# First batch's softmax with tokens on partitions, sums by pairs of heads, six float32 steps

## The chip, the cores and the metric

One core of one Trainium2 chip. The metric is the device time of one execution in microseconds, the median of the runs of the kernel. The engines are named as in the profile: PE is TensorE (PEld its weight loads), DVE is VectorE, ACT is ScalarE, POOL is GpSimd, SP is SyncE, whose queue issues nearly all transfers.

## The reference

Memory attention of 8 batches, 8 heads, 576 tokens, head dimension 64, 32 memories, followed by a feed-forward layer (512 to 2048 to 512) on the 4608 tokens. All in float32.

```python
a = exp(phi - max over the 576 tokens);  a = a / (sum over the tokens + 1e-9)
k_m = einsum('bhsm,bhsd->bhmd', a, k);   v_m = einsum('bhsm,bhsd->bhmd', a, v)
scores = q @ k_m^T / 8;                  attn = softmax over the 32 memories
x = attn @ v_m, heads side by side       # 4608 x 512
h = x @ w_in;  g = h * erf(softplus(h));  out = g @ w_out
```

## The kernel before

The work is a sequence of 128 steps: 8 batches times 16 chunks of 128 of the 2048 hidden columns. For each batch v_m is first multiplied with w_in ("vw"), so that a step's h is one product of the attention weights (`at`, 256 head-memory rows by 576 tokens) with vw. A step consists of:

- `ffn1`: h of the chunk, two halves of 288 tokens (`U`), each 2 float32 matmuls in the first `FR1` = 4 steps ("exact") and 6 afterwards, where each operand is split into a rounded high part and a rest (float32r), three products for each of two groups of 128 rows;
- `softplus` and `erf` on ACT, in groups of four steps, because each needs its own table;
- `g_split` on DVE: g = e*h, and from step `FR2` = 8 on also a high part and a rest of it;
- `ffn2`: g's columns times w_out, added up in four PSUM banks (`pso0` to `pso3`) over the 16 steps of a batch, one float32 matmul for each bank in the first `FR2` steps, three split ones afterwards. The last 64 tokens of two batches are done together (`ffn2_rest`, tile `psr`). `store` copies a bank out on ACT and issues the transfer.

w_in and w_out come as packed 64-bit words (`load_weight`), and `decode` restores float32 with one ACT and two DVE operations; `split_wo` makes the split of w_out for the later steps.

Each operation is put on a list with an engine (or several to choose from), a cost and a rank (`op`). `Plan.order` then simulates the engines with these costs and issues, engine by engine, the ready operation of lowest rank. So the order in each engine's queue is fixed before the run and follows the planner's costs. `at(step)` is 100 times the step; some ranks and engines are corrected by a table of numbers just before the plan is run. Where the planner sees PE idle before the first second product, `fill` puts matmuls of an identity there (tile `idle`, L378). Tiles come from pools of few slots, and an operation waits until a slot is free; PSUM has four slots in the pool `ps`.

The first batch's start, before: the transposed phi is loaded (`phiT`), its maxima, exponentials and sums are taken along the tokens (`phi_sums`), and PE turns the exponentials so that tokens lie on partitions (`numbers_of`). The sums over the tokens for k and v (`sums_and_turn`, L619) are matmuls with phi's 32 columns of one head as weights, four heads beside each other in the array, and k's (or v's) 64 columns streamed. ACT or DVE scales the result by 1/sum while copying it twice (tile `kvk`), PE turns it (L651), and it is copied to `km` or `vm`. Scores (`attention`, L689) have the memories on partitions: km is the weight, q is streamed, 288 tokens in a unit, two units. DVE transposes blocks of 32 by 32 (L737), so that softmax runs over the 32 memories along the free dimension: maximum (L740), subtraction (L742), exp on ACT (L745), sum (L746), reciprocal, product (L751), and the block transposition back (L758) into `at`.

Transfers are issued in the order phiT (two halves), k (two groups), first half of q, first w_in, v (two groups), second half of q, second w_in, first w_out, and so on. q's halves lie in two of the eight slots of the pool `wo`, which the weights take over later.

Of the kernel before, what the change touches and what calls it, by code (L numbers as in the profile page):

```python
# [9 lines left out]
F32 = mybir.dt.float32  # L10
# [21 lines left out]

ROW = 116

PE, DVE, ACT, POOL, SP = "PE", "DVE", "ACT", "POOL", "SP"
# [39 lines left out]
class Plan:  # L75
# [55 lines left out]
    def order(self):  # L131
# [29 lines left out]
        while len(out) < len(self.ops):  # L161
# [70 lines left out]
            for y in x.after:  # L232
                n_wait[y] -= 1
                y.ready = max(y.ready, x.end + self.SIGNAL)
                if not n_wait[y]:
                    for w in y.ways:
                        waiting[w].append(y)
# [10 lines left out]
def tile_memory_attention_then_erf_softplus_ffn(  # L248
# [5 lines left out]
    phi: bass.AP,  # L254
    phiT: bass.AP,
    w_in: bass.AP,
    w_out: bass.AP,
# [27 lines left out]
    LAG = 6  # L285
    FR1, FR2 = 4, 8
    IN_PSUM = 1

    pools = {
# [60 lines left out]
    make_identity(nc, ident)  # L350
    begun = const.tile([P, 1], F32, name="begun")
    rest = const.tile([P, NK, 2, P], F32R, name="rest")
    km = [const.tile([P, NP_, M], F32, name=f"km{i}") for i in range(2)]
# [64 lines left out]
    def load_q(rank, u):  # L418
        b, hf = divmod(u, 2)
        src = qT[b, hf].rearrange("r (p s) -> r p s", p=NP_)  # L420
        if u < 2:
            key = tile_("wo", "q", u, shape=[P, NP_, U], pool="wo")
            load(rank, P * NP_ * U * 4, [key], lambda: nc.sync.dma_start(out=get(key), in_=src))
            return
        for x in range(2):
            key = tile_("at", "q", u, x, shape=[P, 2, U], pool="at")
            load(rank, P * 2 * U * 4, [key], lambda x=x, key=key: nc.sync.dma_start(
                out=get(key), in_=src[:, 2 * x : 2 * x + 2]))

    def q_keys(u):  # L430
        return [("q", u)] if u < 2 else [("q", u, x) for x in range(2)]

    def q_of(u, rows, p):
        return get(("q", u))[rows, p] if u < 2 else get(("q", u, p // 2))[rows, p % 2]

# [101 lines left out]
    def memories(rank, rank_2, b, parts):  # L537
# [5 lines left out]
        else:  # L543
# [5 lines left out]
            for g in range(NG):  # L549
                numbers_of(rank, b, g, range(n, NC), last, g)  # L550
        for turn_n, part in enumerate(parts):
            first, second = sums_and_turn(rank_2 + turn_n * 0.01, b, part)
            together(rank_2 + turn_n * 0.01, first)
            together(rank_2 + turn_n * 0.01, second)

    bundles = []
# [165 lines left out]
    def attention(rank, rank_2, u, more=0):  # L722
# [13 lines left out]
        for g in range(NG):  # L736
# [15 lines left out]
            out=view(), in0=view(), in1=wide(rs), op=ALU.mult))  # L752
        shape = [P, NG, U]
        if u < 2:
            to = tile_("at", "at", u, shape=shape, pool="at")
        else:
            to = tile_("sc", "f", u)
        op(DVE, on_dve(S), rank_2, [s], [to], lambda: nc.vector.transpose(  # L758
            out=get(to).rearrange("p g n -> p (g n)"), in_=get(s).rearrange("p g n -> p (g n)")))
        if u >= 2:  # L760
            at_split(rank_2, u, to)

# [11 lines left out]
    def ffn1(rank, i, half):  # L774
# [4 lines left out]
        part = [(k % 4, par) for par in range(2)]  # L779
        h = ("h", i)  # L780
        if i < IN_PSUM:
            ps = tile_(f"pso{half + 1}", "psh", i, half)
        else:
            if half == 0:
                tile_("h", *h)
            ps = tile_("ps", "psh", i, half, shape=[P, U], pool="ps")

        def emit():
# [10 lines left out]

        op(PE, (2 if exact else 6) * mm(U, exact), rank, [(w, q) for w in ws for q in part] + ats,  # L800
           [ps], emit, holds=[] if i < IN_PSUM else [h])
        if i < IN_PSUM:
            return

        def keep():
            return get(h)[:, half * U : (half + 1) * U]

        op(DVE, on_dve(U), rank - 20, [ps], [(h, half)],
           lambda: nc.vector.tensor_copy(out=keep(), in_=get(ps)),  # L809
           other={ACT: (on_act(U, True), lambda: nc.scalar.activation(keep(), get(ps), AF.Identity))})  # L810

    last = []

    def halves_of(i):

        return [(slice(x * U, (x + 1) * U), ("psh", i, x)) for x in range(2)]

    def softplus(rank, i, edge):
        e = tile_("e", "e", i)
        if i < IN_PSUM:  # L820
            for x, (half, ps) in enumerate(halves_of(i)):
                last[:] = [op(ACT, on_act(U, True), rank, [ps], [(e, x)],
                              lambda half=half, ps=ps: nc.scalar.activation(
                                  get(e)[:, half], get(ps)[:, :U], AF.Softplus),
                              kind="softplus", edge=edge and x == 1, after=last)]
            return
# [8 lines left out]
    def g_split(rank, i):  # L835
# [3 lines left out]
        if i < FR2:  # L839
            t = tile_(("g_hi", "g_lo")[i % 2], "g", i, shape=[P, S], pool="g")  # L840
            if i < IN_PSUM:
                for x, (half, ps) in enumerate(halves_of(i)):
                    op(DVE, on_dve(U), rank, [(e, x), ps], [(t, x)],
                       lambda half=half, ps=ps: nc.vector.tensor_tensor(
                           out=get(t)[:, half], in0=get(e)[:, half], in1=get(ps)[:, :U], op=ALU.mult))
# [27 lines left out]
    def ffn2(rank, i, d):  # L873
# [8 lines left out]
        def emit():  # L882
# [4 lines left out]
           kind="stop filling" if k == 0 else None)  # L887
        if k == NK - 1:
            store(rank, o, [(b * S + d * P, P)])

    def ffn2_rest(rank, b, first, n):
# [14 lines left out]
        if first + n == NK:  # L906
            store(rank, o, [((b + x) * S - REST, REST) for x in range(2)])

    def store(rank, o, rows):
        final = o[1] >= B - 2 if o[0] == "psr" else o[1] == B - 1  # L910
# [3 lines left out]
        for n, (r, ln) in enumerate(rows):  # L914
            e, by = (ACT, nc.scalar) if o == ("psr", B - 1) and n else (SP, nc.sync)
            op(e, 60, rank, [t], [], lambda n=n, r=r, ln=ln, by=by: by.dma_start(
# [34 lines left out]
    decode(at(-3), "in", 0)  # L951
    for u in range(2):
        together(at(-8), attention(at(-8), at(-7 + 2 * u), u))
    together(at(-5), vw(at(-5), 0, 0, 2, FR1 > 0))
# [6 lines left out]
    for c in range(NPR):  # L961
        if c:
            when(2 * c - 3, decode, at(2 * c - 3), "in", c)
            n = at(2 * c - 1.5)
            when(2 * c - 1, lambda n=n, c=c: together(n, vw(n, 0, 2 * c, 2, 2 * c < FR1)))
        when(2 * c, decode, at(second[2 * c] - 2.5), "out", c)
        n = second[16 + 2 * c] - 5 - c if 2 * c < FR2 else second[2 * c] - 2
# [63 lines left out]
    for b in range(1, B, 2):  # L1031
        for k in range(0, NK, 2):
            n = (b + 1) * NK + 2 + k // 4 if b < B - 1 else max(second[NS - NK + k + 1] + 1, NS)
            when(n, ffn2_rest, at(n + 0.6), b, k, 2)
    for k in range(NS):
        when(split_at[k], g_split, at(second[k] - 1.5), k)
        for d in range(NT):
            when(second[k], ffn2, at(second[k] + 0.5), k, d)

# [14 lines left out]
    for n, d in {  # L1054
        104: -18, 161: 366, 162: 366, 180: -354, 217: 211, 229: -211, 253: -495,
    }.items():
        plan.ops[n].rank += d
    for n, e in {103: ACT, 174: ACT}.items():
        plan.ops[n].ways = {e: plan.ops[n].ways[e]}
# [64 lines left out]
```

## Time and profile before

| | |
|---|---|
| median of 3 runs | 705.66 us (705.51 to 705.80) |
| profiled execution | 705.09 us |
| its span, first to last instruction | 703.3 us |
| granted clock of PE, mean | 0.999 |
| PE / PEld / DVE / ACT / POOL busy | 695.2 / 561.2 / 450.1 / 492.1 / 108.7 us |
| bytes moved | 66.71 MB, mean 95 GB/s |

How to read the rows: a timeline row has start, duration, engine, line, operation, output and inputs by the program's names, shapes, count of merged instructions, and in brackets the idle time before it and who ended it. A row of a group has count, busy time and mean nanoseconds of one. A row of stretches has the stretch, its length, and each engine's busy time with its count, then the granted clock, the DMA engines' share and GB/s. A float32 matmul stands in the trace as two records of PE and two of PEld, a float32r one as one of each. A q behind an engine's name is its queue, which issues transfers. Matmul durations overlap, so the distance from start to start tells their cost.

### The profile page before, as it was taken

How to read it: one execution, taken by the hardware profiler on the slowest of the kernel's cores; microseconds unless marked ns; L12 is line 12 of the kernel's file. 1: busy time of each engine (PE TensorE's matmuls, PEld its weight loads, DVE VectorE, ACT ScalarE, POOL GpSimd, SP SyncE). 2: the span in 40 equal slices, each digit the busy share in tenths (PEclk: the TensorE clock that was granted, in tenths of full speed). 3: DMA queues.
4: the chain of work that ended last, by engine and by line, in shares of the span. 5: the costliest groups of instructions: out<-in, count | busy, mean ns of one | idle time of the engine just before them, and what ended most of it. 6: DMA issues, size and time to landing. Idle time of an engine off the chain costs nothing.

```text
span 703.3 us, 12316 instructions
## 1 busy us (share of the span) xinstructions
PE 695.2 (99%) x4858; PEld 561.2 (80%) x4858; DVE 450.1 (64%) x775; ACT 492.1 (70%) x796; POOL 108.7 (15%) x262
## 2 busy tenths in 40 slices
PE   8999999999999999999999999999999999999997
PEld 4665678888887888888888788888888788888886
DVE  4999999678753576775554755765575346745530
ACT  4899989966866777888655876687576555776821
POOL 0031223211110211111111111111111021111110
PEclk9999999999999999999999999999999999999999
DMA  9999130714202041123310323110010100010002
GB/s 362 417 414 416 70 101 3 285 35 180 73 3 81 29 188 41 57 65 104 119 34 1 108 83 140 35 61 1 5 62 4 61 16 1 2 60 1 1 1 75
DMA packets 19849, 66.71 MB, mean 95 GB/s; under 512 B 2256, under 2 KB 2256, under 8 KB 19792
## 3 DMA queue, kind: packets, MB, share of 16 engines
q1 hardware_dynamic: 19424, 64.85, 24.8%
q10 hardware_dynamic: 368, 1.08, 0.4%
q8 instruction: 38, 0.62, 0.4%
q14 instruction: 19, 0.16, 0.1%
HBM read 56.49 MB, written 9.44 MB: 94 GB/s over the span
## 4 chain that ended last, share of the span: by engine, by line
PE 90%; ACT 5%; DMA 3%; DVE 1%; issue 1%; ACTq 0%
PE pso L869 49%; PE psh L792 27%; PE psr L869 6%; PE psa L689 5%; PE psa L619 2%; DMA q<-qT 2%; ACT w L448 1%; ACT e L832 1%; ACT e L827 1%; ACT L832 1%; ACT vw_hi L365 1%; DMA phiT<-phiT 1%; DMA out<-ot 0%; ACT ot L913 0%; PE psa L651 0%
## 5 line engine op out<-in xcount | busy, mean ns | idle before, releaser
L869 PE MATMUL pso<-wo,g_hi 128*128 128x512 f32 x960 | 301.0, 395 | 0.2 <-ACT ot L913 0.2
L869 PEld LDWEIGHTS pso<-wo,g_hi 128*128 128x128 f32 x960 | 171.7, 188 | 44.2 <-issue 12.6
L869 PE MATMUL pso<-wo,g_lo 128*128 128x512 f32 x480 | 188.5, 393 | 0.0
L810 ACT ACTIVATE h<-psh 128x288 f32<-128x288 f32 x175 | 71.4, 409 | 136.9 <-PE psh L792 135.9
L865 POOL CAST rest<-g_hi 128x64 fp32r<-128x64 f32 x120 | 54.9, 458 | 430.7 <-DVE g_hi L860 415.2
L860 DVE CAST g_hi<-e 128x576 fp32r<-128x576 f32 x120 | 53.9, 451 | 95.4 <-PE pso L869 93.7
L792 PE MATMUL psh<-at_hi,vw_hi 128*128 128x288 f32 x496 | 110.1, 303 | 0.3 <-DVE vw_lo L367 0.3
L869 PEld LDWEIGHTS pso<-wo,g_lo 128*128 128x128 f32 x480 | 90.1, 188 | 20.5
L792 PE MATMUL psh<-at_lo,vw_hi 128*128 128x288 f32 x496 | 106.3, 296 | 0.0
L792 PE MATMUL psh<-at_hi,vw_lo 128*128 128x288 f32 x496 | 105.8, 295 | 0.0
L858 DVE TENSOR_TENSOR e<-e,h 128x576 f32<-128x576 f32 x120 | 89.2, 755 | 21.8 <-ACT e L832 21.8
L792 PEld LDWEIGHTS psh<-at_hi,vw_hi 128*128 128x128 f32 x496 | 87.2, 188 | 17.9 <-issue 4.5
L861 DVE TENSOR_TENSOR g_lo<-e,g_hi 128x576 fp32r<-128x576 f32 x120 | 92.6, 772 | 7.6
L827 ACT ACTIVATE e<-h 128x576 f32<-128x576 f32 x127 | 86.0, 684 | 6.0 <-DVE h L809 3.8
L832 ACT ACTIVATE e<-e 128x576 f32<-128x576 f32 x128 | 81.0, 677 | 0.4
L792 PEld LDWEIGHTS psh<-at_hi,vw_lo 128*128 128x128 f32 x496 | 79.8, 188 | 0.0
L792 PEld LDWEIGHTS psh<-at_lo,vw_hi 128*128 128x128 f32 x496 | 79.2, 188 | 0.0
L865 POOL CAST rest<-g_lo 128x64 fp32r<-128x64 f32 x120 | 44.1, 367 | 92.8 <-DVE g_lo L861 89.8
L367 DVE TENSOR_TENSOR vw_lo<-psa,vw_hi 128x512 fp32r<-128x512 f32 (+1 forms) x68 | 40.1, 637 | 15.0 <-ACT vw_hi L365 15.0
L869 PE MATMUL psr<-wo,rest 128*128 128x512 f32 x192 | 49.3, 392 | 0.0
L809 DVE COPY h<-psh 128x288 f32<-128x288 f32 x79 | 35.3, 450 | 16.6 <-PE psh L792 16.1
L365 ACT ACTIVATE vw_hi<-psa 128x512 fp32r<-128x512 f32 (+1 forms) x68 | 34.1, 561 | 12.4 <-PE psa L689 12.3
(81 smaller groups left out, 653.8 us busy)
## 6 DMA issues: line engine op xcount, KB each, us to landing
kv<-kv SPq DMA_DIRECT2D x31, 640.0 KB, 8.3
out<-ot SPq DMA_DIRECT2D x32, 256.0 KB, 2.2
w<-w_in SPq DMA_DIRECT2D x8, 1023.8 KB, 15.0
w<-w_out SPq DMA_DIRECT2D x8, 1023.8 KB, 14.8
q<-qT SPq DMA_DIRECT2D x28, 288.0 KB, 3.2
phi<-phi SPq DMA_DIRECT2D x7, 640.0 KB, 4.4
phiT<-phiT SPq DMA_DIRECT2D x15, 288.0 KB, 3.3
q<-qT SPq DMA_DIRECT2D x2, 576.0 KB, 10.3
```

The lines of the kernel that those rows point to most:

```text
L365: lambda: nc.scalar.activation(get_hi(), get_src(), AF.Identity))
L367: lambda: nc.vector.tensor_tensor(out=get_lo(), in0=get_src(), in1=get_hi().bitcast(F32), op=ALU.subtract))
L792: nc.tensor.matmul(out=get(ps)[:, :U], lhsT=x[:, g, k % 4 * P : (k % 4 + 1) * P], rhs=y[:, g, :], start=(n + g == 0), stop=(n == len(parts ...
L809: lambda: nc.vector.tensor_copy(out=keep(), in_=get(ps)),
L810: other={ACT: (on_act(U, True), lambda: nc.scalar.activation(keep(), get(ps), AF.Identity))})
L827: last[:] = [op(ACT, on_act(S), rank, [("h", i)], [e], lambda: nc.scalar.activation(get(e), get(("h", i)), AF.Softplus), kind="softplus", ...
L832: last[:] = [op(ACT, on_act(S), rank, [e], [e], lambda: nc.scalar.activation(get(e), get(e), AF.Erf), kind="erf", edge=edge, after=last)]
L858: op(DVE, on_dve(S), rank, [e, h], [e], lambda: nc.vector.tensor_tensor(out=get(e), in0=get(e), in1=get(h), op=ALU.mult))
L860: op(DVE, on_dve(S, 1), rank, [e], [hi], lambda: nc.vector.tensor_copy(out=get(hi), in_=get(e)))
L861: op(DVE, on_dve(S), rank, [e, hi], [lo], lambda: nc.vector.tensor_tensor(out=get(lo), in0=get(e), in1=get(hi).bitcast(F32), op=ALU.subtract))
L865: lambda x=x, y=y: nc.gpsimd.tensor_copy(out=rest[:, k, x, cols], in_=get(y)[:, NT * P :]))
L869: nc.tensor.matmul(out=o, lhsT=y, rhs=z, start=(start and n == 0), stop=(stop and n == len(parts) - 1))
```

## The change

- First batch's sums: k's (v's) 128 columns of a pair of heads are the weights, phi's 64 columns of the pair are streamed; the useful blocks lie on the diagonal, so nothing is turned. 1/sum comes from a diagonal matrix multiplied by ones on PE ("every"), copied to SBUF; one DVE operation for each parity of heads and group multiplies and writes km or vm. km is written into a cleared 128 x 256 area beside the first part of q, zero outside the blocks.
- First batch's attention: q comes as 256 and 320 tokens. Three units: 256 tokens (two blocks of 128), 128 tokens, 192 tokens (two blocks of 96). q is the weight and km is streamed, so tokens lie on partitions and softmax needs no block transposition. For unit 0 (`AGAIN`) the scores are computed a second time and minus the maximum is added by a matmul, so that ACT takes exp directly from PSUM; for the other two DVE subtracts. PE turns the result, and ACT or DVE copies it to `at`.
- `FR2` is 6 instead of 8. The exact first products have halves of 256 and 320 tokens, the second in pieces of 32 and 288.
- The last three steps' second products are issued bank by bank (`TAIL`), the last bank is copied in two halves by ACT and DVE and stored through both queues.
- In the planner PE work that follows PE work is ready without the signal's delay; the table of corrected ranks has 50 entries instead of 7, that of engines 7 instead of 2.

```diff
-    FR1, FR2 = 4, 8
+    FR1, FR2 = 4, 6
+    AGAIN = (0,)
+    TAIL = 3
...
+    def first_memories(rank):
...
+        for x in range(2):
+            ps = tile_("ps", "psa", "mem", x, shape=[P, NP_, 2, M], pool="ps")
+            for g in range(NG):
+                def sums(ps=ps, x=x, g=g):
+                    for p in range(2):
+                        for c, ln in enumerate(ROWS):
+                            pair = 2 * g + p
+                            nc.tensor.matmul(
+                                out=get(ps)[:, pair].rearrange("p e m -> p (e m)"),
+                                lhsT=get(("kv", 0, x, g))[:ln, c, p * 2 * D : (p + 1) * 2 * D],
+                                rhs=get(a)[:ln, c, pair * 2 * M : (pair + 1) * 2 * M],
...
+                op(PE, 2 * NC * mm(2 * M, True), rank + x * 0.01, [a, ("kv", 0, x, g)], [(ps, g)], sums)
...
+    def first_attention(rank, rank_2):
...
+        for unit, (t0, n, nc_) in enumerate(((0, P, 2), (2 * P, P, 1), (3 * P, (S - 3 * P) // 2, 2))):
...
+            op(PE, nc_ * NP_ * mm(2 * M, True), rank, [qk] + kms, [ps], scores)
+            op(DVE, on_dve(w), rank_2, [ps], [mx], ... reduce_max ... negate=True
+            if unit in AGAIN:
...
+                op(PE, nc_ * NP_ * mm(2 * M, True), rank_2, [qk] + kms, [ps_2], ... scores(ps_2, False))
+                op(PE, mm(w, True), rank_2, [ps_2, mx], [ps_2], less)
+                op(ACT, on_act(w, True), rank_2, [ps_2], [e], ... AF.Exp
+            else:
+                op(DVE, on_dve(w), rank_2, [ps, mx], [e], ... add
+                op(ACT, on_act(w), rank_2, [e], [e], ... AF.Exp
...
+            op(PE, NG * nc_ * 108, rank_2, [e], [pt], turn)
...
-        op(PE, (2 if exact else 6) * mm(U, exact), rank, [(w, q) for w in ws for q in part] + ats,
+        op(PE, 2 * mm(n, True) + 70 * half if exact else 6 * mm(U, False), rank,
...
+    def halves(i):
+        at_ = 2 * P if i < FR1 else U
+        return slice(0, at_), slice(at_, S)
...
+            if b == B - 1 and k >= NK - 4:
+                n, rank = second[NS - 1], at(second[NS - TAIL] + 0.5) + 10 * (k - NK + 4) / 2 - 0.5
...
+            late = k - (NS - TAIL)
+            when(second[k], ffn2, at(second[k] + 0.5) if late < 0 else at(second[NS - TAIL] + 0.5) + 10 * d + late, k, d)
```

More of the change, by code (lines that the diff above doesn't have):

```diff
@@ L779, in ffn1 @@
         part = [(k % 4, par) for par in range(2)]
-        h = ("h", i)
+        h, c = ("h", i), halves(i)[half]
+        n = c.stop - c.start
         if i < IN_PSUM:
@@ L785, in ffn1, with emit_first @@
                 tile_("h", *h)
-            ps = tile_("ps", "psh", i, half, shape=[P, U], pool="ps")
+            ps = tile_("ps", "psh", i, half, shape=[P, n], pool="ps")
+        def emit_first():
+            x, done = get(ws[0]), 0
+            while done < n:
+                v, a = divmod(c.start + done, U)
+                ln = min(n - done, U - a)
+                for g in range(NG):
+                    nc.tensor.matmul(
+                        out=get(ps)[:, done : done + ln], lhsT=x[:, g, k % 4 * P : (k % 4 + 1) * P],
+                        rhs=get(("at", v))[:, g, a : a + ln], start=g == 0, stop=g == NG - 1)
+                done += ln
         def emit():
@@ L805, in keep @@
         def keep():
-            return get(h)[:, half * U : (half + 1) * U]
-        op(DVE, on_dve(U), rank - 20, [ps], [(h, half)],
+            return get(h)[:, c]
+        op(DVE, on_dve(n), rank - 20, [ps], [(h, half)],
            lambda: nc.vector.tensor_copy(out=keep(), in_=get(ps)),
-           other={ACT: (on_act(U, True), lambda: nc.scalar.activation(keep(), get(ps), AF.Identity))})
+           other={ACT: (on_act(n, True), lambda: nc.scalar.activation(keep(), get(ps), AF.Identity))})
     last = []
+    def halves(i):
+        at_ = 2 * P if i < FR1 else U
+        return slice(0, at_), slice(at_, S)
     def halves_of(i):
-        return [(slice(x * U, (x + 1) * U), ("psh", i, x)) for x in range(2)]
+        return [(x, x.stop - x.start, ("psh", i, n)) for n, x in enumerate(halves(i))]
     def softplus(rank, i, edge):
@@ L820, in softplus @@
         if i < IN_PSUM:
[L821 to L824, printed above, removed]
+            for x, (half, n, ps) in enumerate(halves_of(i)):
+                last[:] = [op(ACT, on_act(n, True), rank, [ps], [(e, x)],
+                              lambda half=half, n=n, ps=ps: nc.scalar.activation(
+                                  get(e)[:, half], get(ps)[:, :n], AF.Softplus),
                               kind="softplus", edge=edge and x == 1, after=last)]
@@ L841, in g_split @@
             if i < IN_PSUM:
[L842 to L845, printed above, removed]
+                for x, (half, n, ps) in enumerate(halves_of(i)):
+                    op(DVE, on_dve(n), rank, [(e, x), ps], [(t, x)],
+                       lambda half=half, n=n, ps=ps: nc.vector.tensor_tensor(
+                           out=get(t)[:, half], in0=get(e)[:, half], in1=get(ps)[:, :n], op=ALU.mult))
             else:
```

169 lines of the change are left out of this document (147 added, 22 removed), and 7 rows, old and new, of the table g.

## The prediction

> **What bounds the kernel now.** I read the page's busy times first, then the chain of waits, then busy times by stretch.
>
> ```profile
> span 703.3 us, 12316 instructions
> PE 695.2 (99%) x4858; PEld 561.2 (80%) x4858; DVE 450.1 (64%) x775; ACT 492.1 (70%) x796; POOL 108.7 (15%) x262
> PE 90%; ACT 5%; DMA 3%; DVE 1%; issue 1%; ACTq 0%
> 22.27:38.97 16.70, 16.16 (x115) 11.13 (x113) 16.63 (x24) 16.32 (x29) 0.00 (x0) 1.00 1.02 415
> 38.97:63.00 24.03, 23.72 (x200) 15.11 (x198) 23.60 (x36) 23.88 (x39) 9.18 (x14) 1.00 1.02 414
> 63.00:110.00 47.00, 46.83 (x292) 32.01 (x291) 46.95 (x75) 40.89 (x65) 10.07 (x13) 1.00 0.35 130
> 0.00:22.27 22.27, 12.47 (x28) 5.59 (x28) 1.00 0.93 375
> ```
>
> The three stretches list PE, PEld, DVE, ACT, POOL, the clock and the DMA; the last row is the filling of L378 alone (PE, PEld). From 38.97 us, the first second product, PE is full. Before 22.27 more than half of what PE does is filling. So the time is the start, plus PE's work, plus the tail; DVE is full too from 22 to 110 us (46.95 of 47.00), which is a second bound close behind. The granted clock is 1.00 throughout. The profiled execution took 705.09 us for its span of 703.3; the median of the runs is 705.66. The sum below starts from 705.09, and 0.57 is added at its end.
>
> The start, in order of time:
>
> ```profile
> 7.96 1.33 PE L619 MATMUL psa<-kv,phi 116*32 116x64 f32 x80
> 10.83 0.29 DVE L678 TENSOR_SCALAR km<-psa 64x128 f32<-64x128 f32 x1 [0.73 <-ACT km L676]
> 10.85 1.04 PE L689 MATMUL psa<-q,km 64*32 64x288 f32 x16
> 11.82 3.49 PE L378 MATMUL idle<-ident 128*128 128x512 f32 x8
> 12.85 0.75 DVE L740 TENSOR_REDUCE smx<-sc 128x18 f32<-128x576 f32 x1
> 16.19 0.77 PE L619 MATMUL psa<-kv,phi 116*32 116x64 f32 x40 [0.17 <-DMA kv<-kv]
> 17.70 0.72 PE L689 MATMUL psa<-q,km 64*32 64x288 f32 x16 [0.75 <-DMA q<-qT]
> 19.16 0.95 PE L689 MATMUL psa<-w_in,vm 64*32 64x256 f32 x16
> 21.39 0.77 DVE L758 STREAM_TRANSPOSE at<-sc 128x576 f32<-128x576 f32 x1
> 22.50 2.10 PE L792 MATMUL psh<-at,vw_hi 128*128 128x288 f32 x8
> 26.27 0.77 DVE L758 STREAM_TRANSPOSE at<-sc 128x576 f32<-128x576 f32 x1
> 27.10 4.15 PE L792 MATMUL psh<-at,vw_hi 128*128 128x288 f32 x16
> 33.70 0.64 PE L792 MATMUL psh<-at_hi,vw_hi 128*128 128x288 f32 x2
> 37.10 0.59 PE L378 MATMUL idle<-ident 128*128 128x256 f32 x2
> 38.97 3.60 PE L869 MATMUL pso<-w,g 128*128 128x512 f32 x8
> ```
>
> The reader sees a chain: k sums, k memories, scores, softmax on DVE, the first product of step 0's first half at 22.50, its second half at 27.10, the first second product at 38.97.
>
> **The part that decides: the price of a narrow float32 matmul.** A float32 matmul is two records, each with its own weight load. The new sums load 128 columns of kv and stream 64 of phi; the new scores load up to 128 tokens and stream 64. No row has that shape. Two rows bound it:
>
> ```profile
> 64.00 0.30 PEld L869 LDWEIGHTS pso<-w,g 128*128 128x128 f32 x2 [0.47 <-issue]
> L869 PEld LDWEIGHTS pso<-wo,g_hi 128*128 128x128 f32 x960 | 171.7, 188 | 44.2 <-issue 12.6
> ```
>
> Low end: the 80 records at 7.96 run four column groups side by side, so 64 columns stream in 1.33/20 = 0.066 us. High end: after a stall two loads of 128 columns take 0.30 with 0.19 each, so the second starts 0.11 after the first, when the first matmul takes its weights over. If that holds here, a record cannot come more often than 0.11, and streaming hides beneath the loading. The second row has the very operation and width, so I take 0.11, that is 0.22 per matmul, and keep 0.13 for the range.
>
> ```profile
> 18.36 0.44 PE L651 MATMUL psa<-ident,kvk 128*128 128x128 f32 x2
> 56.71 0.66 PE L651 MATMUL psa<-ident,kvk 128*128 128x128 f32 x4
> 699.02 0.60 ACT L913 ACTIVATE ot<-psr 128x512 f32<-128x512 f32 x1 [0.76 <-PE psr L869]
> ```
>
> Two turns more take 0.22 more, so one is 0.11; ACT takes 0.60 for 512 columns out of PSUM.
>
> **PE's work to the first second product, at 0.22.** From 7.96: k sums 2 x 2 x 5 = 20 matmuls, 4.4, to 12.3; a wait for the two DVE products into the memory, bounded by 0.29 each (they have half of that row's columns), 0.65 with signals, to 13.0. Unit 0's scores 8 x 0.22 = 1.75; the same again, 1.75; the product that adds minus the maximum, 512 columns in two records of at most 0.45 (3.60/8 in the row at 38.97), 0.9. v sums 4.4. Unit 1's scores 0.87; unit 2's, with 96 columns loaded, 8 x 2 x 0.08 = 1.3. Turns: 10 at 0.11, 1.1. First vw 0.95. That is 25.9 if nothing waits. Then the exact first products of steps 0 to 3. Before: 32 records, 16 of them 4.15, so 8.3 less the drain, 7.8. The new halves are 256 and 320 tokens, the latter as 32 + 288; the columns are the same, but the four records of 32 columns take 0.11 instead of 0.03 each, +0.33 a step, 9.1 in all: 35.0. Two more vw (26.41 to 27.10 and 31.27 to 31.87 now) 1.3, steps 4 and 5 as now (33.70 to 36.96) 3.3, and the 0.9 of the fourth vw with phi's turn: 40.4 against 38.97. So the start is **+1.4**: the PE work added by the change, some 11 us, uses up the filling that it had. Bounds: at 0.13 the chain of DVE decides instead (rival one), -2.0; with a wait in PE's queue +4 (rival two).
>
> The chains beside it at 0.22: unit 0's numbers. Scores end 14.9, maximum over 512 columns 0.67 (0.75 for 576), the added product ends 17.5, exp 0.6, sum 0.67, small ones 0.4, product 0.68, turn and copy 1.2: 21.2, about 1 us ahead of the row at 21.39 + 0.77. This gain is real but covered by PE, which is still at v's sums (they end near 21.7). On DVE the change takes away ten operations of about 0.76 (rows at 12.85 and 21.39), four short transposes and the small ones, some 10.5; it puts in twelve of 0.34 to 0.68 and ten short ones, by the same rows and the 0.29 some 9: an estimate of 1.5 saved.
>
> DMA: q of the first batch keeps its bytes, split 256/320 tokens; the second part still ends the same sum of bytes, so unit 1 cannot start before the 17.70 of now. The k memory lies in the first q's slot; so the third w_out load, which takes that slot over, waits for unit 2's scores, and SP's queue behind it with it:
>
> ```profile
> 22.61 0.33 SPq L399 DMA_DIRECT2D w<-w_out  x1
> w<-w_out SPq DMA_DIRECT2D x8, 1023.8 KB, 14.8
> ```
>
> It is issued at 22.61 and lands 14.8 later, with that much transfer ahead of it, so 2 us of delay are hidden: nothing. Without that backlog they would be paid in full. POOL's clearing of the memory stands where POOL is idle (x0 in the stretch after): nothing; if it came late the products on DVE would wait.
>
> **Six float32 steps, not eight.**
>
> ```profile
> 65.92 3.43 PE pso L869 x8
> 94.08 2.75 PE pso L869 x12
> L860 DVE CAST g_hi<-e 128x576 fp32r<-128x576 f32 x120 | 53.9, 451 | 95.4 <-PE pso L869 93.7
> L861 DVE TENSOR_TENSOR g_lo<-e,g_hi 128x576 fp32r<-128x576 f32 x120 | 92.6, 772 | 7.6
> 121.93 1.22 DVE L367 TENSOR_TENSOR wo<-wf,wo 128x1024 fp32r<-128x1024 f32 x1
> 123.06 0.79 DVE L861 TENSOR_TENSOR g_lo<-e,g_hi 128x576 fp32r<-128x576 f32 x1
> 124.14 0.62 PE L869 MATMUL pso<-wo,g_hi 128*128 128x512 f32 x2
> ```
>
> PE: a float32 step is 3.43, a split one 2.75: 2 x 0.68 = **-1.4**, all of it where PE is full. DVE gets 2 x (0.45 + 0.77) = 2.4 more, and the split of w_out 3 (1.22) comes forward from 121.93 to some 85 us: 3.7 in a stretch where DVE is full, with 0.3 to spare at 123.85 (124.14 less the end of 123.06 + 0.79). Cover: 1.5 saved at the start, and ACT's 6 us of room between 63 and 110, to which the copies of h can go (47.00 less 40.89). Bounds 0 and +2; I take **+0.3**.
>
> **Later waits, ranks, tail.** Of PE's waits after 38.97 the longest are
>
> ```profile
> PEld psh L792 <- DVE vw_lo L367: 0.9, 2, 0.5
> PEld psa L619 <- ACT phi L534: 0.8, 1, 0.8
> 699.65 0.55 ACTq L916 DMA_DIRECT2D out<-ot  x1
> ```
>
> PE comes 1.4 later to them, and the ranks written out are other ones: -0.9 to +0.5, I take **-0.5**. At the end the order of the last three steps changes and no matmul is added; three stores go out earlier, the last copy is two halves of 256 columns instead of 512 (0.60 to about 0.4), queued on ACT and SP as now: -0.6 to 0, **-0.3**. If DVE still had work there, its half would wait.
>
> Sum: +1.4 - 1.4 + 0.3 - 0.5 - 0.3 = -0.5: 704.6, and 0.57 more for the median, 705.1; I give **705.0**. A measurement of this kernel tells about 0.2%, 1.4 us, from no change, so this is called no change.
>
> **Rivals.** One: *the narrow matmuls stream faster than their loads suggest*, 0.13 each or less. Then k sums end at 10.6, unit 0's numbers at 17.9, v (landed by 16.19) sums, first vw and its copy at 20.1, so the first product comes 2.3 earlier than 22.50, the second half near 25.5 instead of 27.10: start -2.0, with the other terms 701.7. For it: the 0.066 of the four groups, and PE's filling of 3.49 at 11.82, which shows room. Against it: the pair of loads. The Trainium skill, "TensorE: Matmul & The Clock Gate", section "Back-to-back issue gap", gives a gap of N/2.4 + 2.5 ns, from which I estimate some 0.056 us for a record of two passes of 64 columns, and by it the sum would be about 701.5; the 0.11 above speaks against it, and no run here shows 64 columns under such a load.
>
> Two, the other side: *a turn stands in PE's queue ahead of the first products*. PE runs in order; the turn of unit 2 waits for DVE's chain on it (0.67 + 0.68 + 0.67 + 0.4 + 0.68, and exp 0.6: 3.7) behind its scores. If unit 2's turn or the sums behind unit 0's stand before the first vw, PE waits 3.7 less the 1.0 that lies between: +2.7, 707.7. It decides as soon as over 1 us of it is not covered. For it: all of it is one queue, and scores have one rank. Against it: PE's filling of 12.47 shows that waiting is planned where it is cheap.
>
> Three: *DVE becomes the bound at steps 12 to 16*, because of its 3.7 more and 0.3 of room: +1.7 instead of +0.3, 706.4. Against it: the room on ACT.
>
> **Chances.** The forecast 0.45 (its own range 703.6 to 706.4: faster 0.15, same 0.25, slower 0.05); rival one 0.25, faster; two 0.15 (slower 0.13, same 0.02); three 0.15 (same 0.09, slower 0.06). Faster 0.40, within 0.2% 0.36, slower 0.24. Range 701.6 to 707.8: it takes in rival one's time and rival two's.
>
> **What the changed profile would show.** The sums: L619's successor with 40 records per memory; starts 0.11 apart, k sums of 4.4 us, mean I right; 2.2 to 2.7, rival one. The first product of step 0 at 24 to 26 us, the first second product near 40. Two steps fewer of float32 records (48 instead of 64), 2.75 for steps 6 and 7. PE waiting for DVE's g_lo between 105 and 125: rival three. PE's load idle before a turn, with DVE's product as releaser, between 18 and 29: rival two. The last store's copy of 256 columns about 4 us before the end. I am wrong if the first second product comes well ahead of 38.97, or later than 42.

## The result, and the profile after

The changed kernel takes 710.84 us (median of 5 runs, 710.73 to 711.09) against 705.66 of the kernel before (705.49 to 705.84): ratio 1.0077, 95% interval 1.0066 to 1.0088. That is 5.2 us slower; 705.0 was forecast, with a range of 701.6 to 707.8. Its profiled execution took 711.09 us for a span of 709.3 us, at a granted clock of 1.00.

From the page, the span, the busy times and the chain:

```profile
span 709.3 us, 12253 instructions
...
PE 701.2 (99%) x4824; PEld 575.6 (81%) x4824; DVE 449.0 (63%) x781; ACT 496.8 (70%) x805; POOL 106.0 (15%) x264
...
PE 94%; DVE 3%; ACT 2%; issue 0%; POOL 0%; POOLq 0%
```

PE is busy 99% of the time, as before. This share hides what happened, since PE's own filling and its matmuls' slow pitch count as busy. The timeline of PE up to the first second product tells more (start, duration, engine, line, output and inputs, count, idle time before):

```profile
9.05 4.58 PE L595 MATMUL psa<-phi,kv 116*128 116x64 f32 x40
...
14.30 3.78 PE L851 MATMUL psa<-q 128*128 128x64 f32 x32 [0.40 <-issue]
...
18.83 4.58 PE L595 MATMUL psa<-phi,kv 116*128 116x64 f32 x40
...
23.24 2.42 PE L851 MATMUL psa<-q 128*128 128x64 f32 x24
...
28.55 1.13 PE L942 MATMUL psh<-at,vw_hi 128*128 128x256 f32 x4 [0.33 <-ACT at L906]
...
30.60 1.67 PE L386 MATMUL idle<-ident 128*128 128x512 f32 x4
...
46.78 3.70 PE L1035 MATMUL pso<-w,g 128*128 128x512 f32 x8
```

These are the k sums, unit 0's scores (twice), the v sums, the other units' scores, the first product of step 0 (22.50 before), a filling, and the first second product (38.97 before). Forty records of 64 columns take 4.58, so one starts every 0.11 us. The first second product is 7.8 us later, where 1.4 was forecast.

DVE in the same stretch, and then the whole stretch from the first instruction to the first second product (its length, PE, PEld, DVE, ACT, POOL, clock, DMA share, GB/s):

```profile
13.74 0.95 DVE L611 SCALAR_TENSOR_TENSOR q<-psa,bias 64x64 f32<-64x64 f32 x4 [5.38 <-PE psa L595]
...
16.33 0.69 DVE L859 TENSOR_REDUCE smx<-psa 128x16 f32<-128x512 f32 x1 [1.64 <-PE psa L851]
...
23.44 0.48 DVE L611 SCALAR_TENSOR_TENSOR vm<-psa,bias 64x64 f32<-64x64 f32 x2 [3.82 <-PE psa L595]
...
23.95 0.69 DVE L879 TENSOR_REDUCE ssm<-sc 128x16 f32<-128x512 f32 x1
...
42.46 0.49 DVE L971 COPY h<-psh 128x320 f32<-128x320 f32 x1 [0.48 <-PE psh L942]
```

```profile
0.00:46.78 46.78, 42.85 (x318) 33.66 (x318) 29.46 (x58) 24.70 (x45) 0.99 (x8) 1.00 0.98 397
```

The kernel before, DVE's first operation on scores and its only longer wait behind it, then the whole stretch:

```profile
11.97 0.85 DVE L737 STREAM_TRANSPOSE sc<-psa 128x288 f32<-128x288 f32 x2 [0.84 <-PE psa L689]
...
18.50 0.85 DVE L737 STREAM_TRANSPOSE sc<-psa 128x288 f32<-128x288 f32 x2 [1.09 <-PE psa L689]
```

```profile
0.00:38.97 38.97, 35.86 (x363) 21.26 (x363) 28.80 (x49) 25.66 (x48) 0.70 (x6) 1.00 0.97 392
```

DVE does 29.46 us of work to that point, 28.80 before: about the same. But it waits 5.38 us for the k sums, 1.64 for the scores and 3.82 for the v sums. From its first operation on scores to the first second product DVE is full in both kernels, but for these waits:

| | before | after | difference |
|---|---|---|---|
| first operation of DVE on scores | 11.97 | 16.33 | +4.36 |
| idle from there to the first second product | 1.09 | 3.82 + 0.48 | +3.21 |
| work in that stretch | 25.91 | 26.15 | +0.24 |
| first second product | 38.97 | 46.78 | +7.81 |

The work is the stretch less its idle time. Counted from the beginning of the k sums, which is 1.09 later itself (9.05 for 7.96), the beginning of DVE's work on the scores is 3.27 later. From the first second product to the end of the last matmul it is 658.9 us now (to 705.7) and 660.0 before (to 698.98): -1.1. From there to the end of the span it is 3.6 and 4.3: -0.7. Sum +6.0, the difference of the two profiled spans; the medians differ by 5.2.

### The profile page after: what moved, and what is told of

Same layout as the page of the kernel before. It is cut to its first block, busy times and chain, and to the rows that moved or that the text cites. A ratio compares the mean times of both kernels' runs of the same rounds, so it can differ in the third digit from the quotient of the medians.

```text
span 709.3 us, 12253 instructions
## 1 busy us (share of the span) xinstructions
PE 701.2 (99%) x4824; PEld 575.6 (81%) x4824; DVE 449.0 (63%) x781; ACT 496.8 (70%) x805; POOL 106.0 (15%) x264
## 3 DMA queue, kind: packets, MB, share of 16 engines
q10 hardware_dynamic: 432, 1.08, 0.4%
## 4 chain that ended last, share of the span: by engine, by line
PE 94%; DVE 3%; ACT 2%; issue 0%; POOL 0%; POOLq 0%
PE pso L1035 49%; PE psh L951 27%; PE psr L1035 6%; PE psa L750 5%; PE psa L680 2%; PE psh L942 1%; PE psa L595 1%; PE idle L386 1%; PE psa L851 1%; ACT w L462 0%; DVE g L1013 0%; PE psa L712 0%; DVE w L465 0%; DVE w_in L489 0%; DVE h L971 0%
## 5 line engine op out<-in xcount | busy, mean ns | idle before, releaser
L1035 PE MATMUL pso<-wo,g_hi 128*128 128x512 f32 x976 | 306.9, 396 | 0.0
L1035 PEld LDWEIGHTS pso<-wo,g_hi 128*128 128x128 f32 x976 | 174.6, 188 | 45.5 <-issue 16.4
L1035 PE MATMUL pso<-wo,g_lo 128*128 128x512 f32 x488 | 191.7, 393 | 0.0
L972 ACT ACTIVATE h<-psh 128x288 f32<-128x288 f32 (+1 forms) x182 | 74.1, 409 | 125.5 <-PE psh L951 124.7
L1031 POOL CAST rest<-g_hi 128x64 fp32r<-128x64 f32 x122 | 52.4, 431 | 430.5 <-DVE g_hi L1026 410.4
L1035 PEld LDWEIGHTS pso<-wo,g_lo 128*128 128x128 f32 x488 | 91.6, 188 | 21.0
L951 PE MATMUL psh<-at_hi,vw_hi 128*128 128x288 f32 x496 | 108.3, 300 | 0.2 <-DVE vw_lo L375 0.2
L971 DVE COPY h<-psh 128x288 f32<-128x288 f32 (+1 forms) x72 | 31.8, 448 | 24.4 <-PE psh L951 23.6
L1035 PE MATMUL psr<-wo,rest 128*128 128x512 f32 x192 | 46.1, 390 | 0.0
```

The lines of the kernel that those rows point to most:

```text
L951: nc.tensor.matmul(out=get(ps)[:, :U], lhsT=x[:, g, k % 4 * P : (k % 4 + 1) * P], rhs=y[:, g, :], start=(n + g == 0), stop=(n == len(parts ...
L972: other={ACT: (on_act(n, True), lambda: nc.scalar.activation(keep(), get(ps), AF.Identity))})
L1031: lambda x=x, y=y: nc.gpsimd.tensor_copy(out=rest[:, k, x, cols], in_=get(y)[:, NT * P :]))
L1035: nc.tensor.matmul(out=o, lhsT=y, rhs=z, start=(start and n == 0), stop=(stop and n == len(parts) - 1))
```

## The experiments

Two theories of the late start were tried. Theory A: in-order queues, laid out by a planner that has a narrow float32 matmul at half its price, make engines wait for each other. Its rival, B: PE's added work is itself the bound. A third, D, came out of them: DVE is the bound. Differences below are medians against the kernel before, run beside it on the same chip; the changed kernel stands at +5.2. Where traces are compared, the first second product is counted from the beginning of the k sums (46.78 - 9.05 = 37.73), because that beginning itself moves by up to 0.5 between executions.

**The price.** Under the same load of 128 columns the sums stream the 128 columns of two pairs instead of the 64 of one; the other pair's are not used.

```diff
-    rhs=get(a)[:ln, c, pair * 2 * M : (pair + 1) * 2 * M],
+    rhs=get(a)[:ln, c, g * P : (g + 1) * P],     # out: 128 columns instead of 64
```

> The changed kernel, but each of the first batch's sums streams all 128 columns of its group of phi instead of the pair's 64, under the same load of 128 columns; the extra products are not used. Load theory (0.11 us a record is the time to load 128 columns): 40 records still take about 4.6 us, starts 0.11 apart, time within 0.5 us of the changed kernel. Stream theory: starts 0.17 apart or more, 40 records in 6.8 us, time 3 us or more above it.

```profile
8.94 4.63 PE L595 MATMUL psa<-phi,kv 116*128 116x128 f32 x40
```

4.63 for 40 records, against 4.58: twice the columns cost nothing, so the load of the weights sets the pitch. Its only execution took 711.33. The pitch follows the loaded columns: from start to start it is 0.111 with 128 of them and 0.085 with 96 (unit 2's scores). The Trainium skill, "TensorE: Matmul & The Clock Gate", section "Back-to-back issue gap", gave 0.056 by my estimate, from the formula that the section gives for an isolated matmul and that, as it says itself, leaves out the loading of weights. The trace does not agree with that estimate, and the measurement decides.

**New plans.** Three kernels changed what the planner sees: its price of the narrow matmuls made true; the six float32 steps alone put into the kernel before; the v products made to wait for unit 0's product.

```diff
-    op(PE, 2 * NC * mm(2 * M, True), ...        # and the same for the scores
+    op(PE, 2 * NC * 228, ...                    # 190 where 96 columns are loaded
```
```diff
-    FR1, FR2 = 4, 8
+    FR1, FR2 = 4, 6
```

> The changed kernel, with one thing altered: the planner's cost of a float32 matmul that streams 64 columns is 228 ns (190 with 96 columns loaded) instead of 112, and that of a second exact half is 340 ns more than by its columns instead of 70. No operation is added or removed; orders and filling may differ. Queue theory (the loss comes from orders and filling made for matmuls at half their price, so that DVE and PE stand in front of the wrong work): most of the 3.9 us in which PE waits or fills between 25.7 and 34.0 us goes, first second product near 43.5 instead of 46.8, time about 707.5. Work theory (PE simply has too much to do in the start, orders matter little): first second product 46 or later, time 710 to 711.

> The kernel before with FR2 = 6 instead of 8 and nothing else. If the term of the prediction holds (-1.4 us of PE's work, with DVE's 3.7 us more mostly covered): 704.2 to 704.7. If DVE is the bound at steps 12 to 16: 705.7 or more, and PE waits for g_lo between 100 and 125 us. If the loss of the changed kernel sits here: 708 or more.

> The changed kernel, with one dependency added: DVE's four products that write vm come after unit 0's product with 1/sum, so that unit 0's sum no longer stands behind them (it was ready at 19.6 us and began at 23.95). Queue theory: unit 0's sum begins at 19.7, its turn on PE right after the scores at 25.7, the first product at about 27.3 instead of 28.55, time 1.0 to 1.3 below the changed kernel, about 709.7. Work theory: the turn is early but vw sets the start, time within 0.4 of the changed kernel.

They took 725.45, 729.18 and 715.80 us: +20.0, +23.7 and +10.3, far from every size that was expected. Each one made a new order of all 128 steps, for which the corrected ranks, given by operation number, were not made. The longest wait of PE in the first and the second (from their lists of waits), and the clock around the second's:

```profile
PE pso L1035 <- DVE g_hi L1026: 4.6, 1, 4.6
```
```profile
PE psa L689 <- DMA q<-qT: 10.5, 1, 10.5
```
```profile
114.80:118.20 3.40, 1.51 (x20) 0.58 (x20) 0.33 (x2) 2.09 (x7) 0.00 (x0) 1.00 0.79 270
118.20:128.69 10.49, 0.01 (x2) 0.03 (x1) 6.60 (x11) 1.36 (x2) 0.00 (x0) 0.50 0.98 369
128.69:132.00 3.31, 3.31 (x32) 0.97 (x32) 2.08 (x5) 1.74 (x4) 0.00 (x0) 0.52 0.89 289
```

So their times say nothing of the edited part. In the first the start can be read by itself: with the true price in the planner the first second product comes at 46.48, 37.8 from the k sums, no earlier than in the changed kernel, though in another order. The kernels that follow keep the order of every queue as it was planned and move only the operations named.

**Moving work in the queues.** First DVE's numbers of unit 0 go ahead of the v products; then also the decode of the second w_in ahead, and vw of steps 2 and 3.

```diff
+    move(sum, reciprocal, product of unit 0  -> ahead of the v products)      # DVE
+    move(turn of unit 0 -> ahead of unit 1's scores; its copy -> ahead of unit 1's exp)
```
```diff
+    move(decode of the second w_in -> ahead on ACT, and ahead of the v products on DVE)
+    move(vw of steps 2 and 3 -> ahead of unit 2's turn); three fillings dropped
```

> The changed kernel with every queue's order kept and one thing moved: DVE's sum, reciprocal and product of unit 0 stand ahead of its two products into the v memory, PE's turn of unit 0 ahead of unit 1's scores, ACT's copy ahead of unit 1's exp. Theory A (the changed kernel loses its time to in-order queues that were laid out for matmuls at half their price): the first product of step 0 comes near 27.3 us instead of 28.55, the first second product 1.0 to 1.3 earlier than 46.78, the time 709.5 to 710. Theory B (PE's work itself, 0.22 us for each narrow matmul, sets the start, and the waits only show what would be filled anyway): no gain, 710.8 within 0.3.

> As the run before, and moreover the decode of the second w_in stands ahead of the first batch's maxima and exponentials on ACT and ahead of the v products on DVE, vw of steps 2 and 3 stands ahead of unit 2's turn on PE, and the three planned fillings beside them are dropped. Theory A: dense work of PE begins near 32.2 instead of 33.97, first second product 43.5 to 45, time 708 to 709. Theory B: 710.8 within 0.5, since what is not waited for here is waited for at the next step.

Measured: 709.96 (+4.8) and 709.28 (+4.1). The first second product comes at 45.61 and 44.85, 0.9 and 1.5 earlier when counted from the k sums (8.75 and 8.65). The first time is as expected, the second 0.3 above. Theory A is right in direction, and small: it accounts for 1.5 of the 6.7 us by which the start is longer (37.73 against 38.97 - 7.96 = 31.01).

**Less work on PE.** Unit 0's scores once instead of twice.

```diff
-    scores(ps_2, False); less = matmul that adds minus the maximum            # PE
+    tensor_tensor(out=e, in0=scores, in1=-max, op=add)                         # DVE
```

> As the run before, and unit 0's scores are not computed a second time: DVE adds minus the maximum into SBUF, as for the other units (PE gives up 8 narrow matmuls and one of 512 columns, 2.6 us; DVE gets one operation of about 0.7). Theory A with PE's work as the bound of the start: another 1.5 to 2.5, time 706 to 707. If DVE's chain on unit 0 is the bound by then: another 0 to 0.5.

> As the run before, and the k sums stand ahead of phi's later turns on PE as soon as their operands are there, one filling less before them: they begin near 8.0 us instead of 9.05. Theory A: another 0.9 to 1.1, time 705 to 706. If v's landing (14.56) or the second w_in's (18.64) sets the end of the start by then: 0 to 0.3.

Measured: 711.49 (+6.3) and 712.56 (+7.4), both slower than the kernel they start from, which neither theory expected. In the last one the k sums did not start earlier but at 9.23, since a small product that waits for ACT now stood ahead of them. The surprise is the clock (stretches of r3; the third number from the end is the granted clock):

```profile
15.90:20.50 4.60, 4.60 (x42) 4.48 (x41) 4.34 (x5) 0.63 (x1) 0.00 (x0) 1.00 1.01 413
20.50:24.00 3.50, 2.06 (x16) 2.08 (x16) 3.36 (x6) 1.73 (x2) 0.00 (x0) 0.84 1.02 424
24.00:27.90 3.90, 3.39 (x31) 2.39 (x30) 3.45 (x10) 0.84 (x3) 0.00 (x0) 0.50 1.00 414
```
```profile
21.95 0.63 PE L898 MATMUL psa<-ident,sc 128*128 128x128 f32 x4 [1.44 <-DVE sc L891]
```

PE stood idle for 1.44 us, and its clock went to half for about 10 us: four records of 128x256 took 2.08 instead of 1.13. This is the slowest of the four executions (712.29). In one of the others the mean clock is 1.00, and it took 711.78, more than the two at 0.995 (711.19 and 711.20); so the clock alone does not explain the loss. The next kernel puts 1.08 us of filling into that gap.

```diff
+    turn of unit 0: fill = 5
```

> r3 again, with 5 filling matmuls of 128 columns (1.08 us) ahead of PE's turn of unit 0, in the stretch 20.52 to 21.95 in which r3's PE stood idle before its granted clock fell to 0.50. Theory C (the clock: an idle stretch of PE of about 1.4 us costs half the clock for the following 10 us; the second scores had been keeping PE busy): the clock stays at 1.00, 64 columns under a load of 128 stay at 0.11 us, the first second product comes 3 us or more earlier than in r3, the time 707 to 708.5. Rival (taking away PE work cannot help because DVE's chain bounds the start, and the clock would fall anyway): the clock falls again, 711 to 712.

```profile
20.50:24.00 3.50, 3.18 (x25) 2.54 (x25) 3.36 (x6) 0.60 (x1) 0.00 (x0) 1.00 1.01 421
24.00:27.90 3.90, 2.92 (x32) 1.79 (x30) 3.74 (x12) 1.07 (x4) 0.00 (x0) 1.00 1.01 418
```

The clock stays at 1.00, and the first second product comes at 45.21, 36.25 from the k sums, instead of 37.85. That part of theory C holds, though 1.6 us and not 3. But the start is no earlier than with the second scores (36.20), though PE has 2.6 us less of the kernel's own work (and DVE 0.7 more). So theory B does not hold for this work. The time, 711.20 (+5.9), lies where the rival had put it, though the clock did not fall; it is worse than with the second scores for the most part for another reason:

```profile
PE pso L1041 <- ACT ot L1101: 1.1, 1, 1.1
```

At 228 us ACT's copy of a result waits for an earlier store to land, and PE for that copy; this wait is not in the changed kernel, nor with the second scores. It also stands, with 0.9 to 1.3 us, in the two kernels before this one and in the next. Why the store lands later is not settled.

One more order: all of unit 0's numbers ahead of the first w_in's decode. In this kernel unit 0's exponential came to stand behind its sum and product, so unit 0's values differ and DVE does not wait for it.

```diff
+    move(sum to product of unit 0 -> ahead of the decode of the first w_in)
+    move(decode of the second w_in on DVE -> behind unit 2's numbers)
+    move(vw of steps 2 and 3 -> behind the second halves of steps 0 and 1)
```

> r3 with three more moves: DVE's sum to product of unit 0 ahead of the decode of the first w_in (the turn can then follow the v sums at once, near 20.5), the decode of the second w_in on DVE behind all of unit 2's numbers, and vw of steps 2 and 3 on PE behind the second halves of steps 0 and 1; 9 filling matmuls ahead of unit 2's turn. Theory A with DVE as the bound of the start (about 12.4 us of DVE work between the end of the v sums and step 2's weights): first product near 24.6, no drop of the clock, first second product 42.5 to 44, time 706.5 to 708. If PE's work alone bounded it: first second product 42.5 or earlier. If a clock drop remains: over 709.

710.66 (+5.3), 2.7 above the upper end expected. The first product comes at 24.45, as expected, 4.1 earlier than in the changed kernel; the first second product at 45.21, 36.46 from the k sums, 1.2 later than the upper end expected. Part of this the edit made itself, with its fillings ahead of unit 2's turn (DVE's product of unit 2, the fillings on PE, and DVE's copy behind the turn):

```profile
27.17 0.69 DVE L891 TENSOR_TENSOR sc<-sc,srs 96x512 f32<-96x512 f32 x1
...
27.22 2.10 PE L386 MATMUL idle<-ident 128*128 128x512 f32 x6
...
29.69 0.56 DVE L913 COPY at<-psa 128x384 f32<-128x384 f32 x1 [1.83 <-PE psa L898]
```

The product was done at 27.86, but the turn began at 29.16, behind the fillings, and DVE idled 1.83 us for it. So this run does not show how much an early first product alone is worth. From 29.69 to the first second product DVE has no further wait, while PE waits 2.2 us in four places.

**Is DVE the bound?** The plainest test adds work to it. One kernel issues unit 0's maximum twice, ahead of the 3.82 us in which DVE idles; another issues unit 2's maximum and sum twice, where DVE is full. A third shortens the k sums.

```diff
+    twice: the maximum of unit 0, 0.69                       # d1
+    twice: the maximum 0.68 and the sum 0.68 of unit 2       # d2
+    if x == 0 and c in (1, 2): continue                      # d3, in the sums
```

> The changed kernel with its order kept, unit 0's maximum on DVE issued twice (0.69 us more, at 17.0, in a stretch in which DVE then idles 3.82 us before the v sums' end). Theory D (DVE is full from the first maximum to the first second product and sets the start; its idle time is free): first second product at 46.8, time 710.8, both within 0.2. If every DVE operation cost its time wherever it stands: +0.7.

> The changed kernel with its order kept, unit 2's maximum (0.68) and its sum (0.68) on DVE issued twice, at 26.9 and 29.2, where DVE is full: 1.36 us more. Theory D: first second product 1.1 to 1.4 later than 46.78, time 711.9 to 712.2. If PE's work sets the start (dense from 33.97) and DVE only follows: 0 to 0.3.

> The changed kernel with its order kept, the k sums over 3 of the 5 blocks of tokens only (so the memories are those of 352 tokens): 16 records of 0.111 less, 1.8 us, ahead of DVE's first maximum. Theory D: the maximum, the v sums' end and the first second product come 1.6 to 1.8 earlier, time 709.0 to 709.3. Rival (v's landing at 14.56, q's second part at 16.15 and the second w_in at 18.64 set the chain): 0 to 0.6.

| | first second product from the k sums | time | against before |
|---|---|---|---|
| changed kernel | 37.73 | 710.84 | +5.2 |
| 0.69 more in the idle stretch | 46.48 - 8.76 = 37.72 | 710.79 | +5.2 |
| 1.36 more in the full stretch | 47.64 - 8.60 = 39.04 | 712.12 | +6.6 |

The rows of PE in these two kernels, the one with the idle stretch first:

```profile
8.76 4.58 PE L595 MATMUL psa<-phi,kv 116*128 116x64 f32 x40
...
46.48 3.70 PE L1035 MATMUL pso<-w,g 128*128 128x512 f32 x8
```
```profile
8.60 4.58 PE L595 MATMUL psa<-phi,kv 116*128 116x64 f32 x40
...
47.64 3.70 PE L1035 MATMUL pso<-w,g 128*128 128x512 f32 x8
```

The operation in the idle stretch shortens DVE's wait for the v sums from 3.82 to 3.10:

```profile
23.15 0.47 DVE L611 SCALAR_TENSOR_TENSOR vm<-psa,bias 64x64 f32<-64x64 f32 x2 [3.10 <-PE psa L595]
```

It costs nothing, and 1.36 us in the full stretch cost 1.31 and 1.4. So DVE's work from 23.44 on sets when the start ends, while PE, with its fillings, only looks full. This was tested at 26 to 30 us; from 33.97 to 45.8 PE of the changed kernel runs almost without a gap as well, and no run tells there which of the two sets the pace. The kernel with shorter k sums (k sums, unit 0's maximum, first second product):

```profile
8.75 2.79 PE L597 MATMUL psa<-phi,kv 116*128 116x64 f32 x24
...
14.25 0.69 DVE L861 TENSOR_REDUCE smx<-psa 128x16 f32<-128x512 f32 x1 [1.65 <-PE psa L853]
...
44.69 3.70 PE L1037 MATMUL pso<-w,g 128*128 128x512 f32 x8
```

The maximum of unit 0 and the first second product both come 2.1 earlier (14.25 for 16.33, 44.69 for 46.78), of which 0.3 is an earlier beginning of the sums; 1.8 was the time taken out. The price of the k sums goes straight through to the start, and the landings of v, q and the second w_in, its rival, do not hold it up. The time fell by 0.5 only (710.21, +4.7), since the late store shows again, with a wait of 1.3 at 228 us.

**The six float32 steps.** Measured in both directions: two split steps put into the kernel before, and two float32 steps put back into the changed kernel.

```diff
+    if 6 <= i < 8: 3 operations on DVE, 12 float32r matmuls of 512 columns     # f8, kernel before
```
```diff
+    if 6 <= i < 8: 1 operation on DVE, 4 float32 matmuls                       # f10, changed kernel
```

> The kernel before with its order kept, steps 6 and 7 issued as split ones: three operations of DVE instead of one, and 12 float32r matmuls of 512 columns instead of 4 float32 matmuls (operands: g's own tile, so these two steps give other values; the split of w_out is not brought forward). The prediction's term: 2 x 0.68 = 1.4 less on PE, so 704.1 against 705.5; with DVE as the bound there (0.29 of room, 2.4 us more of DVE work): no gain or up to 1 slower.

> The changed kernel with its order kept, steps 6 and 7 done as float32 steps again: 4 float32 matmuls instead of 12 float32r ones on PE, one DVE operation instead of three (w_out's high part alone is used there). If the six-step term of the prediction was gained here (-1.4, since DVE had been relieved by the late start): 712.0 to 712.3. If DVE set these steps as it did in the kernel before (+2.0 there): 709 to 710.8.

In the kernel before: 707.36, +2.0 (ratio 1.0037, 1.0025 to 1.0050), where up to 1 slower was expected. The order of the queues is one planned for a single operation of DVE. PE's part is there (12 records in 2.88 instead of 3.60 for 8, first row), but two waits take its place (PE's waits from 60 to 120 us):

```profile
80.07 2.88 PE L874 MATMUL pso<-g 128*128 128x512 f32 x12
```
```profile
PE psa L689 <- DVE w_in L475: 2.0, 1, 2.0
PE psh L792 <- ACT h L810: 1.1, 1, 1.1
```

In the changed kernel: 712.11, +6.6, so undoing the step costs 1.4 and the step gains 1.4 there. So splitting these two steps costs 2.0 in one kernel and gains 1.4 in the other (the first edit leaves out the split of w_out). The likely reason is the room that DVE has. The stretch of 24 us behind the first second product in the changed kernel (the one of the kernel before stands in the prediction):

```profile
46.78:70.80 24.02, 23.42 (x199) 14.58 (x192) 22.27 (x34) 23.62 (x40) 8.19 (x12) 1.00 0.72 268
```

DVE has 1.75 us of room there, against 0.43 before (23.60 of 24.03), and the transfers are through earlier (268 GB/s for 414): PE is later, so the weights' decode is further on. By this reading the late start paid for the cover of the six steps; no run varied DVE's room alone, and in the 24 us behind these DVE has hardly any room either (23.91 of 24.00, and 24.00 in the kernel before).

**The tail alone,** in the kernel before.

```diff
+    last three steps bank by bank; last bank copied in halves by ACT and DVE, stored through both queues
```

> The kernel before with its order kept up to the last three steps, whose second products are issued bank by bank, the last 64 tokens' sums behind the first bank, and the last bank copied in halves by ACT and DVE and stored through both queues: the tail part of the change alone. The prediction's term was -0.3 (bounds -0.6 and 0); the traces of before and after (4.3 against 3.6 us from the last matmul's end to the end of the span) say -0.7. So 704.8 to 705.2 against 705.5, on the edge of what can be told.

704.60 against 705.35, ratio 0.9989, 0.9980 to 0.9998 (11 runs): 0.75 faster, with bounds of 0.1 and 1.4. It is the only version that is faster than both kernels. Its last copies:

```profile
699.26 0.38 ACT L918 ACTIVATE ot<-pso 128x256 f32<-128x256 f32 x1 [1.46 <-PE pso L869]
...
699.67 0.35 ACTq L923 DMA_DIRECT2D out<-ot  x1
699.68 0.42 DVE L919 COPY ot<-pso 128x256 f32<-128x256 f32 x1 [11.52 <-ACT ot L918]
```

The halves ran one after the other: DVE was released by ACT's copy (in the changed kernel it is ACT that waits for DVE's). So not even all of the gain that the halves offer was had; why they do not run beside each other is not settled.

## Why the prediction was wrong

The step that failed is the start: +1.4 was summed along PE, and +7.8 came, because the start ran along DVE. The terms in their order:

- *The price of a narrow float32 matmul*: right. 0.11 was taken from one pair of loads, and 0.111 was measured. Rival one, the faster stream, is refuted by the doubled columns.
- *PE's work to the first second product*: right in size. Forecast from 7.96 to 40.4 less 0.65 of waits, 31.8 us. The distances between the starts of PE's rows from the k sums to the first second product, without fillings and waits, sum to 32.1 of 37.73, and to 19.6 of 31.01 before. The rest is 3.6 of filling and 2.0 of waits, and was 10.0 and 1.3 before. So PE still had filling left when the start was 6.7 longer.
- *"That is 25.9 if nothing waits"*, and *"This gain is real but covered by PE"*: this step failed. The sum ran along PE and gave the 10 us of filling to the new work, as if filling were room. PE was filling because the chain ran through DVE, and DVE full from 22 us on (16.63 of 16.70) stood in a row that I quoted and read as "a second bound close behind". At the start it was the first. The new matmuls lie ahead of DVE's work, not beside it: k sums of 4.58 instead of 1.33, and scores, move its beginning from 11.97 to 16.33 (1.1 of it because the k sums begin at 9.05 and not at 7.96, behind a product for 1/sum and a filling; the sum had kept 7.96); then it idles another 3.82 while the v sums run. The shortened k sums and the doubled operations show this. The first product came at 28.55 for 25.9 and the first second product at 46.78 for 40.4; of these 6.4 us, 1.1 is the later beginning of the k sums, 1.6 came ahead of the first product and 3.7 behind it, where the sum let PE go on without a wait for DVE's numbers of unit 2 and its decode of the second w_in.
- *"an estimate of 1.5 saved" on DVE*: wrong. To the first second product it works 29.46 instead of 28.80 us. It issues 58 operations there instead of 49: the products into the memories, the copies to `at` and the short ones took what the transpositions gave.
- *Six float32 steps, -1.4 and +0.3*: right in the changed kernel (1.4 by undoing it), but not for the reason given. The cover named, 1.5 saved on DVE and room on ACT, was not there: in the kernel before two split steps lose 2.0. The late start probably made the room.
- *Later waits -0.5*: with the two terms before, -1.6 was forecast from the first second product to the last matmul, -1.1 came.
- *Tail -0.3*: -0.7 in the traces, -0.75 measured alone.
- *Rival two* had the right sign and kind, work that stands ahead in an in-order queue, but the wrong place: not PE's turn, but DVE's v products and ACT's exponentials. Moving work ahead of them gains 1.5, not the whole. *Rival three*, DVE as the bound, was placed at steps 12 to 16; it held for the start.
- *The third w_out load* is issued at 25.09 instead of 22.61, 2.5 later (2 were forecast), and costs nothing, as said: the transfers stay at 397 GB/s through the start (392 before).

Not settled: of the 6.7 us by which the start is longer, 1.5 went with queue orders. The other 5.2 are put down to DVE's late beginning and the rest of its waits, but no order was found that fills DVE's wait for the k sums, and nothing was tried that gives part of DVE's work to another engine.

## What to carry to other kernels

When an engine fills its idle time, or looks 99% busy, look for the engine that is full behind the first result, and sum the chain along that one. Here it was DVE: what delayed its beginning (the k sums) came through in full, and 2.6 us of work taken from PE beside it gained nothing. Test this by doubling one cheap operation in an idle and in a full stretch. And before trying a part of a change alone in a planned kernel, freeze the order, since a new plan of all steps cost 5 to 24 us here against the kernel that it started from, and hid every part.

## What was not expected of the hardware

- A float32 record of PE starts every 0.111 us when 128 weight columns are loaded, every 0.085 with 96, when 64 columns are streamed. Under the load of 128 it makes no difference whether 64 or 128 are streamed (40 records: 4.58 and 4.63).
- Behind an idle gap of 1.44 us in PE its granted clock went to 0.50 for some 10 us, although PE had work for most of them; with 1.08 us of filling in the gap the clock stayed at 1.00. The Trainium skill, "TensorE: Matmul & The Clock Gate", section "Part 1: The HAM clock gate", names an idle window of about 3.4 us as what brings the slow clock; here a gap of less than half of that stood before the drop. The length of one gap does not decide it, though: in the kernel before with two split steps PE idled 2.01 us, and the clock behind it is 1.00 (first the matmul that ends the gap, then the stretch behind it):

```profile
71.92 0.67 PE L689 MATMUL psa<-w_in,vm 64*32 64x256 f32 x16 [2.01 <-DVE w_in L475]
```
```profile
71.94:88.00 16.06, 16.06 (x94) 12.31 (x94) 16.06 (x26) 14.10 (x21) 1.65 (x3) 1.00 0.09 33
```

  What decides is not settled. Filling, or a second computation of scores that need not be done, kept the clock up here; what that is worth in time is not shown (+6.3 without the filling, +5.9 with it).
- In the six steps' new plan the clock is 0.50 through an idle gap of 10.5 us and 0.52 in the 3.3 us after it. It fell as the gap began: in the 3.4 us before, PE is busy for 1.51 us in all and the clock still 1.00. So that gap did not bring it down.
